# Batches 3 to 7 in runs of nine tokens, their attention products on four array quadrants, in a new order

## The chip, the core and the metric

The kernel runs on one core of a Trainium2 chip. A core has five engines with instruction streams of their own: TensorE (PE; its weight loads are shown apart as PEld), VectorE (DVE), ScalarE (ACT), GpSimd (POOL) and SyncE (SP), and sixteen DMA engines that move data between the chip's memory (DRAM) and SBUF. Matmul results go to PSUM, eight banks of 128 partitions by 512 float32. The metric is the device time of one execution in microseconds (us); a kernel's time is the median of several runs.

## The reference

Two stages follow each other: a linear attention without softmax, normalised per head, and a two-layer network with a leaky activation.

```python
kv = np.einsum('bhsd,bhse->bhde', k, v)        # 8 batches, 8 heads, 576 tokens, 64 dims
out = np.einsum('bhsd,bhde->bhse', q, kv)
rms = np.sqrt(np.mean(out * out, axis=-1, keepdims=True) + 1e-06)
attn = (out / rms * g_norm).astype(np.float32)
x = np.ascontiguousarray(attn.transpose(0, 2, 1, 3)).reshape(4608, 512)
h = x @ w_in                                   # 512 -> 2048
g = np.maximum(h, 0.0) + alpha * np.minimum(h, 0.0)
return (g @ w_out).astype(np.float32)          # 2048 -> 512
```

All inputs and the output are float32 in DRAM; the kernel computes in float16 with float32 sums.

## The kernel before

**Windows and batches.** The network runs over nine windows of 512 tokens (w = 0 to 8, four tiles of 128). A batch has 576 tokens, so windows and batches do not line up: window 3 holds the end of batch 2 and the start of batch 3, and so on. Batches 0 to 2 (below `B_NAT`) go through paths of their own in the first 66 us; the change is about batches 3 to 7.

**Loads.** A batch's q, k and v are loaded by POOL with a cast to float16 into one stage tile each, which every later batch uses again. 512 tokens go as four neighbouring tokens per partition (`load_main`, 128 partitions, runs of 1 KB in DRAM); the remaining 64 tokens go by a load of their own into a small buffer (`load_rem`, runs of 256 B). q comes in two halves by heads. Each load may be held back on POOL by a gate, a one-element copy that waits for a given result.

**Order within a batch.** `place_of` says where a token stands: in batches with an odd number the first 64 tokens are the remainder, in even ones the last 64. Output tokens are permuted accordingly, and `row_pieces`, `grid` and `store_rows` put them back when stored.

**kv product** (`kv_mm`, line 1376): for each of four pairs of heads and each of five token groups, one 128-row matmul per head; the two heads go to the two column halves of the array, 40 matmuls of 128x64 a batch. `kv_copy` (ACT) casts the result into `kv_masked`, once straight and once with partition halves exchanged.

**Transposes of q** (`dma_t`, line 397): SP issues DMA transposes that turn q into `qt_sb`, four of 128x512 from the stage tile and one of 64x512 from the remainder.

**Row products** (`rows_mm`, line 567): for two tiles of a window at a time, q times kv. The contraction is 64 long, so a matmul uses one row half (`half`) of the array; consecutive matmuls alternate between the halves. A tile of main tokens takes 8 matmuls of 64 rows by 128 tokens by 64; a part of 64 remainder tokens takes 8 of its own. ACT then squares 8 pieces per tile (line 627), takes the reciprocal root (637), DVE scales the rows (653, `x_rows`) and SP turns them by DMA into `xt` (665), the input of the network.

**The network.** Groups of four matmuls: `h_ps` (lines 687 and 720, 512 columns wide) for the first layer, `yX`, `yY`, `yZ` (line 940, 256 wide) for the second; some first-layer blocks are computed with seven products instead of eight (`mX`, `mY`, `mV`, line 1286), as the second layer's are.

**The order.** From 66 us on, the instruction stream is written out by hand in a list, `ORDER`. Names in it: `ld.k.4.0` is a load (batch 4, part 0; `@` names its gate), `q.3.2` transpose 2 of batch 3, `kv.7` and `kvc.7` the kv product and its casts, `R.3.1` and `R.3.3` the row products of window 3 for tiles (1, 0) and (3, 2), `q2`/`q3` squares, `rs` reciprocal roots, `n` scaling, `x.3.3` the turn of tile 3 of window 3 into `xt`, `M.w.u` and `Ma.w.0` first-layer groups (`Ma.w.0` and `M.w.0` are one group split in two, since the last tile comes later), `p.w.n.k` second-layer groups, `f.w.s.n` first-layer products, `y` evacuations, `st` stores, `S`, `t` and `a` sums on DVE. Each engine takes its own instructions in the list's order and waits for what they need.

Of the kernel before, what the change touches and what calls it, by code (L numbers as in the profile page):

```python
# [17 lines left out]
def kernel(  # L18
# [11 lines left out]
    nc = tc.nc  # L30
# [103 lines left out]
    mask32 = const_p.tile([P, P], FP32, name="mask32")  # L134
    nc.vector.memset(mask32[:], 0.0)
    nc.vector.memset(mask32[0:64, 0:64], 1.0)
    nc.vector.memset(mask32[64:128, 64:128], 1.0)
    mask16 = const_p.tile([P, P], FP16, name="mask16")
    nc.vector.tensor_copy(out=mask16[:], in_=mask32[:])
    eps_t = const_p.tile([P, 1], FP32, name="eps_t")  # L140
    nc.vector.memset(eps_t[:], 1e-6)
    PAD = P // 2
    qt_sb = [const_p.tile([P, NPAIR, PAD + S + PAD], FP16, name=f"qt_sb{i}") for i in range(2)]
    for t in qt_sb:
        nc.vector.memset(t[:, :, 0:PAD], 0.0)
        nc.vector.memset(t[:, :, PAD + S : PAD + S + PAD], 0.0)

# [12 lines left out]
    NBUF = 3  # L160
    HH = H // 2
    bufs = []
    for i in range(NBUF):
        t = {}
        for nm in ("k", "v", "q") if i < 2 else ("k", "v"):
            n = NT if nm == "q" and i == 0 else 1
            t[nm] = qkv_p.tile([P, n, H, D], FP16, name=f"{nm}sb{i}")
            if i > 0 or nm == "v":
                clears.append(t[nm][REM:P, n - 1, :, :])
        bufs.append(t)  # L170
# [29 lines left out]

    def load_main(b, nm, h0=0, h1=H):
# [9 lines left out]
    def load_q(b, i):  # L211
        load_main(b, "q", i * H // QL, (i + 1) * H // QL)

    def buf_of(b, nm):
        return bufs[b % (2 if nm == "q" else NBUF)][nm]

    def rem_of(b, nm):
        return buf_of(b, nm)[:, TPP if nm == "q" and b % 2 == 0 else 0, :, :]
# [170 lines left out]
    def dma_t(b, ts=tuple(range(NT))):  # L389
        qt = qt_sb[b % 2][:, :, PAD : PAD + S]  # L390
        for t in ts if b >= B_NAT else ():
            n = P if t < TPP else REM
            if t == TPP:
                src = rem_of(b, "q")[0:REM].rearrange("p h d -> p (h d)")
            else:
                src = stages[b, "q"][:, 2 * t : 2 * t + 2].rearrange("p h t d -> p (h t d)")
            nc.sync.dma_start_transpose(
                out=qt_flat(b)[:, t * W : t * W + NC * n].rearrange("p (c n) -> p c n", c=NC),
                in_=src,
            )  # L400
# [12 lines left out]
    def place_of(b, r):  # L413
        if b >= B_NAT and b % 2:
            r = r - REM if r >= REM else r + MAIN
        return divmod(r, P) if r < MAIN else (TPP, r - MAIN)
# [1552 lines left out]
```

## Time and profile before

| what | us |
|---|---|
| median of 3 runs | 272.28 |
| lowest, highest run | 271.85, 273.44 |
| the profiled execution | 271.0 |
| its span, first to last instruction | 269.1 |
| TensorE busy in it | 262.0 |
| VectorE, ScalarE, GpSimd busy | 225.7, 192.3, 85.1 |

The span is what the trace shows; the execution's own time adds what lies before and after. A profile page has numbered parts: busy times, the span in 40 slices, DMA queues, the chain of work that ended last, groups of instructions, DMA issues. A group's line reads: line, engine, operation, output<-inputs, shape, count, then busy us, mean ns of one, and idle time of the engine before them with what ended it. A view of waits reads: engine, what it was about to do, what it waited for, total us, times, longest. A matmul's record (some 190 ns at least) is longer than its share of the array, as matmuls overlap; what one costs is read from how the starts follow each other.

### The profile page before, as it was taken

What the parts mean: (1) busy time and instruction counts of PE and PEld (TensorE: products, weight loads), DVE (VectorE), ACT (ScalarE), POOL (GpSimd) and SP (SyncE); (2) the same over time, 40 slices, a digit from 0 to 9 for tenths busy, and PEclk for the clock granted to TensorE, in tenths of its full rate; (3) what the DMA queues carried; (4) which work ended last, traced back from release to release, by engine and by line L of the source; (5) the groups of instructions that cost most, each with busy time, mean ns of one, the idle gap of its engine ahead of it and who ended that gap; (6) DMA issues with size and microseconds to landing.
All of it is one profiled execution on the core that took longest, in us unless ns stands there. A gap on an engine that the chain in (4) does not pass through costs nothing.

```text
span 269.1 us, 6703 instructions
## 1 busy us (share of the span) xinstructions
PE 262.0 (97%) x2477; PEld 183.1 (68%) x2477; DVE 225.7 (84%) x437; ACT 192.3 (71%) x689; POOL 85.1 (32%) x146
## 2 busy tenths in 40 slices
PE   6999999999999999999999999999999999999994
PEld 2554454456666566886788578866886688678894
DVE  7559966899964998999977997899899988979973
ACT  2567637786579878997889779869988885657500
POOL 8943651513132119411905143511020002401400
PEclk9999999999999999999999999999999999999999
DMA  7999999995989899999999969997550101600233
GB/s 194 198 202 206 196 198 189 181 186 96 225 97 189 126 112 134 177 119 133 175 148 109 129 130 167 105 195 145 117 100 19 23 20 38 204 16 2 78 119 117
DMA packets 75460, 35.75 MB, mean 133 GB/s; under 512 B 42516, under 2 KB 73252, under 8 KB 75428
## 3 DMA queue, kind: packets, MB, share of 16 engines
q0 software_dynamic: 41744, 23.68, 63.7%
q1 hardware_dynamic: 32980, 10.90, 24.7%
q10 hardware_dynamic: 704, 0.75, 0.9%
q8 instruction: 19, 0.31, 0.5%
q14 instruction: 13, 0.11, 0.2%
HBM read 36.71 MB, written 9.44 MB: 171 GB/s over the span
## 4 chain that ended last, share of the span: by engine, by line
PE 87%; DMA 4%; DVE 4%; ACT 2%; SPq 1%; issue 1%; DVEq 0%
PE h_ps L687 25%; PE yY L940 15%; PE yX L940 9%; PE yZ L940 9%; PE mY L1286 8%; PE y L732 5%; PE mV L1286 4%; DMA qt_sb<-qst 3%; PE mX L1286 2%; PE h_ps L720 2%; PE or_ps L567 2%; PE kv_ps L1376 2%; DMA y_sb<-in_g_norm_dram 1%; ACT sq_sb L627 1%; DVE gt L1353 1%; PE ssq_ps L492 1%
## 5 line engine op out<-in xcount | busy, mean ns | idle before, releaser
L687 PE MATMUL h_ps<-xt,w_in_sb 128*128 128x512 f16 x348 | 84.0, 379 | 0.0
L702 DVE SCALAR_TENSOR_TENSOR gt<-m_sb,beta_sb,h_ps 128x512 f16<-128x512 f32 x96 | 68.5, 744 | 12.3 <-ACT m_sb L696 11.5
L696 ACT ACTIVATE m_sb<-h_ps 128x512 f32<-128x512 f32 x96 | 55.4, 605 | 20.7 <-PE h_ps L687 14.8
L940 PEld LDWEIGHTS <-s 128*128 128x128 f16 x496 | 47.9, 98 | 9.5
L687 PEld LDWEIGHTS <-w_in_sb 128*128 128x128 f16 x348 | 33.0, 98 | 31.2 <-issue 0.3
L940 PEld LDWEIGHTS <-gt 128*128 128x128 f16 x384 | 37.3, 98 | 7.2
L627 ACT ACTIVATE sq_sb<-or_ps 128x64 f16<-128x64 f32 x192 | 40.8, 261 | 1.6 <-PE or_ps L567 1.1
L627 ACT ACTIVATION_READ_ACCUMULATOR sq_sb<-or_ps 128x1 f32 x192 | 40.1, 247 | 0.0
L940 PE MATMUL yX<-w_out_sb,gt 128*128 128x256 f16 x256 | 36.8, 273 | 0.0
L940 PE MATMUL yY<-wsum,s 128*128 128x256 f16 x256 | 33.5, 273 | 0.0
L744 POOL DMA_DIRECT2D out_dram<-y_sb x31 | 18.3, 597 | 26.7 <-ACT y_sb L996 16.2
L744 POOL DMA_DIRECT2D out_dram<-y_more x11 | 6.6, 601 | 50.7 <-DVE y_more L1002 30.6
L653 DVE TENSOR_TENSOR x_rows<-or_ps,rstd_r 128x512 f16<-128x512 f32 x27 | 18.2, 686 | 4.2 <-ACT rstd_r L637 3.6
L1353 DVE SCALAR_TENSOR_TENSOR gt<-m_sb,beta_sb,mh 128x256 f16<-128x256 f32 x48 | 20.9, 480 | 0.5 <-ACT m_sb L1346 0.4
L1308 DVE TENSOR_TENSOR mh<-mV,mu 128x512 f32<-128x512 f32 x24 | 16.5, 690 | 5.6 <-ACT mu L1305 3.2
L1448 POOL COPY gate_sb<-gt 1x1 f16<-1x1 f16 x19 | 4.1, 216 | 47.8 <-DVE gt L702 37.4
L940 PE MATMUL yZ<-wsum,s 128*128 128x256 f16 x120 | 17.1, 273 | 0.0
L1305 ACT COPY mu<-mY 128x512 f32<-128x512 f32 x24 | 14.4, 602 | 3.7 <-PE mY L1286 3.7
L1346 ACT ACTIVATE m_sb<-mh 128x512 f32<-128x512 f32 x24 | 15.3, 646 | 2.1 <-DVE mh L1308 2.1
L940 PE MATMUL yY<-wsum,gt 128*128 128x256 f16 x128 | 16.6, 272 | 0.0
L732 PE MATMUL y<-w_out_sb,gt 128*128 128x512 f16 x64 | 16.3, 380 | 0.0
L940 PE MATMUL yZ<-w_out_sb,s 128*128 128x256 f16 x120 | 16.0, 273 | 0.0
(151 smaller groups left out, 433.2 us busy)
## 6 DMA issues: line engine op xcount, KB each, us to landing
kst<-in_k_dram POOLq DMA_DIRECT2D x7, 512.0 KB, 8.3
vst<-in_v_dram POOLq DMA_DIRECT2D x6, 512.0 KB, 8.4
qst<-in_q_dram POOLq DMA_DIRECT2D x10, 256.0 KB, 5.6
w_out_sb<-in_moe_w_out_dram POOLq DMA_DIRECT2D x8, 256.0 KB, 12.2
out_dram<-y_sb POOLq DMA_DIRECT2D x7, 256.0 KB, 4.4
out_dram<-y_sb POOLq DMA_DIRECT2D x12, 128.0 KB, 4.4
out_dram<-y_sb SPq DMA_DIRECT2D x5, 256.0 KB, 2.5
w_in_sb<-in_moe_w_in_dram POOLq DMA_DIRECT2D x2, 512.0 KB, 10.7
```

The source lines that it names most:

```text
L627: nc.scalar.activation(out=sq[:, half, j], in_=o_ps[:, half, j], func=AF.Square, accum_out=ssq[:, half, j : j + 1],)
L653: nc.vector.tensor_tensor(out=xr[:].rearrange("p j h d -> p h j d"), in0=o_ps, in1=rstd[:].unsqueeze(3).to_broadcast([P, 2, NPAIR, D]), op ...
L687: nc.tensor.matmul(out=h_ps[:], lhsT=w_in_blk(c, g), rhs=xts[w][:, c, :], start=(c == 0), stop=(c == NC - 1),)
L696: nc.scalar.activation(out=neg[w, g][:], in_=h_ps[:], func=AF.Relu, scale=-1.0)
L702: nc.vector.scalar_tensor_tensor(out=gts[w, i][:, r, :], in0=neg.pop((w, g))[:], scalar=beta_sb[:, g : g + 1], in1=h_ps[:], op0=ALU.mult, ...
L732: nc.tensor.matmul(out=y[:], lhsT=gt_cols(w, g, a * P, (a + 1) * P), rhs=w_out_blk(g), start=(n == 1), stop=(n == NF),)
L744: engs[store_turn[0] % len(engs)].dma_start(out=dst, in_=src)
L940: nc.tensor.matmul(out=bank, lhsT=lhs, rhs=rhs, start=fresh, stop=(c == NK - 1), skip_group_check=True,)
L1286: nc.tensor.matmul(out=t[bank][:, r, :], lhsT=lhs[:, c, r * P : (r + 1) * P], rhs=rhs[:, c, :], start=(fresh and c == r == 0), stop=(c == ...
L1308: nc.vector.tensor_add(out=h_tile(t, what)[:, :, HW:W], in0=src[:], in1=u[:])
L1346: nc.scalar.activation(out=dst, in_=h, func=AF.Relu, scale=-1.0)
L1353: nc.vector.scalar_tensor_tensor(out=gts[w, i][:, r, cols], in0=m, scalar=beta_sb[:, g : g + 1], in1=h, op0=ALU.mult, op1=ALU.add,)
```

## The change

Batches 3 to 7 are loaded like batch 0: the 128 partitions of a pair of heads each take nine neighbouring tokens of one head (64 partitions per head), 2304 B in one run, in two halves per tensor (`load_runs`). There is no remainder load any more. q's stage tile has a tenth, empty run (zeroed once), so that its 128 x 2560 elements turn in five full transposes. A token's place is now a slot (0 to 8, its run position in `SLOTS`) and a partition (0 to 63).

The kv product takes 64-row matmuls: nine runs, two pairs (column half `c`), two heads (row half `i`), twice, 72 matmuls of 64x64 that go round the four quadrants; the two row halves write to two PSUM banks. Row products take 64 tokens a matmul; a part's slot parity gives its row half, its place in the tile (0 or 64) its column half, and the four parts of two tiles take turns. The slots of the four parts are two even and two odd in all pairs of whole tiles from batch 3 on but one: tiles 3 and 2 of window 7 have slots 8, 8, 4 and 6.

Stores of these batches go in pieces of 64 tokens; where the two tiles of a store have neighbouring slots, two tokens go together. The mask is built in float16, the zero columns beside `qt_sb` are gone, and `ORDER` is written anew. A row product now needs all five transposes of its batch, a load of q all five of the batch before.

```diff
+    def load_runs(b, nm, i):
+        if (b, nm) not in stages:
+            first = nm not in kept
+            stages[b, nm] = stage_for(b, nm, [P, NPAIR, (T0 + (nm == "q")) * D])
+            if nm == "q" and first:
+                nc.vector.memset(stages[b, nm][:, :, T0 * D :], 0.0)
+        n = NPAIR // QL
+        nc.gpsimd.dma_start(
+            out=stages[b, nm][:, i * n : (i + 1) * n, 0 : T0 * D],
+            in_=srcs[nm][b].rearrange("h s d -> (h s d)").rearrange(
+                "(j q r) -> q j r", j=NPAIR, r=T0 * D
+            )[:, i * n : (i + 1) * n, :],
+        )
...
             nc.sync.dma_start_transpose(
-                out=qt_flat(b)[:, t * W : t * W + NC * n].rearrange("p (c n) -> p c n", c=NC),
-                in_=src,
+                out=qt_flat(b)[:, t * W : (t + 1) * W].rearrange("p (c n) -> p c n", c=NC),
+                in_=stages[b, "q"][:].rearrange("p j n -> p (j n)")[:, t * W : (t + 1) * W],
             )
...
+    SLOTS = {
+        3: (8, 0, 2, 1, 3, 4, 6, 5, 7), 4: (0, 2, 1, 3, 4, 6, 5, 7, 8), 5: (8, 5, 7, 0, 2, 1, 3, 4, 6),
+        6: (5, 7, 0, 2, 1, 3, 4, 6, 8), 7: (8, 0, 2, 1, 3, 4, 6, 5, 7),
+    }
...
-                        lhs = qt_flat(b)[part, c : c + n]
-                        rhs = kvs[b][part, half ^ h, j, :]
+                        c = (NT * j + t // 2) * P + h * P0
+                        lhs = qt_flat(b)[part, c : c + P0]
+                        rhs = kvs[b][part, (j + half) % 2, 2 * h + j // 2, :]
...
-        apart = all(len({y[0] for y in x}) == 1 for x in ops)
+        apart = all(x[0] >= B_NAT for i in tiles for x in row_parts(w, i))
+        queues = {}
         for x, i in enumerate(tiles):
-            ots[w, "r", i] = o_ps[:, half] if apart else o_ps[:, :, x]
+            ots[w, "r", i] = o_ps[:, x] if apart else o_ps[:, :, x]
+            for op in row_ops(w, i):
+                half, h, rows, n = op[0], op[1], op[2], op[2].stop - op[2].start
+                key = (rows.start, x) if apart else half
+                rank = 0 if apart else (n, half == h, h) if n < P else (n, 0, 0)
+                queues.setdefault(key, []).append((rank, x, op))
+        queues = [sorted(queues[k], key=lambda y: y[0]) for k in sorted(queues)]
...
+        for n in range(max(map(len, queues))):
+            for y in queues:
...
+    def kv_runs(b):
+        kv_tiles[b] = row_tile([2, H, D], "kv_ps")[:, :, 0 : NPAIR // 2, :]
+        for m in range(NPAIR // 2):
+            for t in range(T0):
+                for c in range(2):
+                    for i in range(2):
+                        k_rows, v_rows = (
+                            stages[b, nm][i * P0 : (i + 1) * P0, 2 * m + c, t * D : (t + 1) * D]
+                            for nm in "kv"
+                        )
+                        nc.tensor.matmul(
+                            out=kv_tiles[b][c * D : (c + 1) * D, i, m, :], lhsT=k_rows, rhs=v_rows,
+                            start=(t == 0), stop=(t == T0 - 1), skip_group_check=True,
+                        )
...
-                needs += [("q", b, x) for x in ((TPP,) if t == TPP else range(TPP) if b >= B_NAT else (t,))]
+                needs += [("q", b, x) for x in ((t,) if b < B_NAT else range(NT))]
...
-            own = ()
-            if nm == "q":
-                n = TPP // QL
-                own = (("q", b - 2, t),) if t == TPP else tuple(("q", b - 1, n * t + i) for i in range(n))
+            own = tuple(("q", b - 1, x) for x in range(NT)) if nm == "q" else ()
...
-            store_engines[0] = (nc.scalar if h == 0 else nc.sync,)
+            store_engines[0] = (nc.scalar, nc.sync)
             store_rows(w * W + P, y_sb[:, 1, half], HC + h * P, HC + (h + 1) * P)
```

The new list's stretches that the prediction speaks of:

```
late.2.0 late.2.2 late.2.1 y.1.seed M.2.1 kv.3 r.2.1 S.1.1.2 M.2.2 s.2.1 S.1.1.1 p.1.2.3
ld.v.4.1@s.2.1 S.1.1.0 r.2.2 M.2.3 a.2.2 kvc.3 s.2.2 M.2.5 S.1.1.3 M.2.6 S.1.2.3 q.3.2 r.2.5
S.1.2.0 S.1.2.2 p.1.6.0 s.2.5 r.2.6 Ma.2.0 q.3.1 S.1.2.1 M.2.0 s.2.6 p.1.6.1 p.1.6.2 q.3.4
p.1.6.3 M.2.10 y.1.u2 q.3.0 r.2.0 M.2.9 r.2.3 s.2.0 p.1.7.0 q.3.3 a.3.4 p.1.7.1 s.2.3
p.1.7.2 p.1.7.3 ld.k.4.0@s.2.6 M.2.4 y.1.u3 y.1.c11 M.2.7 r.2.4 r.2.10 p.2.1.0 s.2.4 r.2.7
p.1.4.0 S.1.4.1 r.2.9 ld.q.4.1@s.2.4 R.3.1 s.2.10 p.1.4.1 q2.3.1 S.1.4.0 p.2.1.1 s.2.9
p.1.4.2 q2.3.0 ld.q.4.0@s.2.5 S.2.3.0 M.2.13 q3.3.1 S.1.4.2 s.2.7 M.2.8 q3.3.0
ld.v.4.0@s.2.2 M.2.11 rs.3.1 rs.3.0 n.3.1 r.2.8 M.2.14 r.2.11 n.3.0 s.2.11 R.3.3 x.3.0
p.1.4.3 q2.3.2 s.2.8 M.2.15 S.1.4.3 y.1.c21 x.3.1 p.2.1.2 q3.3.2 p.1.5.0 p.1.5.1 q2.3.3
p.1.5.2 rs.3.2 p.1.5.3 q3.3.3 n.3.2 M.2.12 y.1.c22 x.3.2 rs.3.3 p.2.1.3 r.2.13 n.3.3 p.1.3.0
y.2.p1 p.1.3.1 s.2.13 x.3.3 r.2.12 p.1.3.2 S.2.1.0 r.2.14 p.2.2.0 s.2.12 p.1.3.3 q.4.2
p.2.2.1 y.1.c12 R.4.1 S.2.2.0 Ma.3.0 y.2.seed q.4.3 r.2.15 S.2.3.1 p.2.6.0 q2.4.0 p.2.6.1
s.2.15 q.4.0 M.3.0 M.3.1 q2.4.1 s.2.14 ld.k.4.1@s.2.15 t.3.1 r.3.0 M.3.2 q.4.1 S.2.1.1 r.3.1
...
p.5.6.1 t.6.2 r.6.7 x.7.1 S.5.2.1 kv.7 s.6.1 p.5.6.2 kvc.7 st.3.c12 p.5.6.3 s.6.4 p.5.2.1
s.6.6 y.5.u2 R.7.3 S.5.3.0 M.6.5 st.4.c12 q2.7.2 S.5.3.1 p.5.2.2 q2.7.3 t.6.3 x.7.0 p.5.2.3
```

More of the change, by code (lines that the diff above doesn't have):

```diff
@@ L156 @@
         )
-    NBUF = 3
     HH = H // 2
[L162 to L170, printed above, removed]
+    bufs = {}
+    for b in range(1, B_NAT):
+        for nm in "kvq":
+            n = NT if nm == "q" and b == 2 else 1
+            t = bufs[b, nm] = qkv_p.tile([P, n, H, D], FP16, name=f"{nm}sb{b}")
+            if n == 1:
+                clears.append(t[REM:P, 0, :, :])
     def clear(n):
@@ L534, in row_ops @@
                 for h in range(2):
-                    n = rows.stop - rows.start
-                    half = h if b < B_NAT or t == TPP else t % 2
+                    half = h if b < B_NAT else t % 2
                     part = slice(half * D, (half + 1) * D)
```

286 lines of the change are left out of this document (123 added, 163 removed).

## The prediction

> **What bounds the kernel now.** I read the page first: shares of the engines, the 40 slices and the shares of the chain that ended last.
>
> ```profile
> PE 262.0 (97%) x2477; PEld 183.1 (68%) x2477; DVE 225.7 (84%) x437; ACT 192.3 (71%) x689; POOL 85.1 (32%) x146
> ...
> PE   6999999999999999999999999999999999999994
> ...
> DMA  7999999995989899999999969997550101600233
> ...
> PE 87%; DMA 4%; DVE 4%; ACT 2%; SPq 1%; issue 1%; DVEq 0%
> ```
>
> TensorE is full from the second slice to the last but one, at full clock (the 1.00 in the counts further down). A transfer or a slower neighbour costs time only where it leaves TensorE without work; a saved matmul counts directly. The view of waits, for PE alone, says how much there is to win:
>
> ```profile
> PE warm_ps L316 <- DVE y_sb L133: 1.5, 1, 1.5
> PE alpha_ps L1061 <- DMA y_sb<-in_g_norm_dram: 0.7, 1, 0.7
> PE kv_ps L1376 <- DVE gt L702: 0.5, 1, 0.5
> PE or_ps L567 <- DVE x_rows L653: 0.4, 1, 0.4
> PE or_ps L567 <- DMA qt_sb<-qst: 0.3, 1, 0.3
> ```
>
> The first two belong to the start, before the edited part, and alpha_ps waits for a DMA that the edit leaves alone. So all that waiting costs in the middle is three waits, 0.5 + 0.4 + 0.3 = 1.2 us, each ahead of an attention block. The blocks, and the units of work around them, stand in the chain in order of time (start, us, what; h_ps and yY in their groups of four matmuls):
>
> ```profile
> 69.10 0.86 PE h_ps L687 x4
> ...
> 77.62 6.91 DMA qt_sb<-qst
> ...
> 88.29 0.82 ACT sq_sb L627 x8
> ...
> 99.75 0.44 PE yY L940 x4
> 100.19 0.75 PE kv_ps L1376 x40
> ...
> 184.39 0.60 PE or_ps L567 x24
> ```
>
> A kv product costs 0.75 us, five of them (batches 3 to 7) are edited. Nine of the twelve row blocks of windows 3 to 8 have 16 matmuls, three have 24 (0.60 us each). A block of 16, from the chain cut to 165 to 182 us:
>
> ```profile
> 170.31 0.34 PE or_ps L567 x16
> ```
>
> **Matmuls on quadrants.** A kv product becomes 72 matmuls of 64x64 instead of 40 of 128x64; a row block 32 instead of 16. Whether that costs anything depends on the pace when all four quadrants take turns. No kv product before does that, but the 24-blocks do in places: there 64 tokens are computed on both row halves into both column halves. Counting the matmuls of line 567 begun from 184.30 on (us, PE busy and count, clock, DMA):
>
> ```profile
> 184.30:184.41 0.11, 0.09 (x10) 1.00 0.95 335
> 184.30:184.44 0.14, 0.12 (x14) 1.00 1.03 366
> ```
>
> From 0.41 to 0.44 four are begun in 30 ns: 7.5 ns each at four quadrants. The other bound is the pace of two column halves, line 1376 counted from 66.60:
>
> ```profile
> 66.60:66.72 0.12, 0.06 (x4) 1.00 0.77 73
> 66.60:66.82 0.22, 0.16 (x10) 1.00 1.05 49
> ```
>
> 6 in 0.10 us, 16.7 ns each. I take 7.5, since that row shows the very form. With 0.12 us for entering and leaving a block (0.75 less 38 times 16.7 ns), kv is 72 x 7.5 ns + 0.12 = 0.66 us, 0.09 less: 5 x -0.09 = **-0.4**. At 16.7 ns it is 1.32 us, +2.9 in all.
>
> Row blocks: 32 x 7.5 ns + 0.12 = 0.36 against 0.34, nine of them: +0.2. The block of window 5's tiles 3 and 2 goes from 0.60 to 0.36: -0.2. Window 3's tiles 1 and 0 keep 24 matmuls. Window 7's tiles 3 and 2 are the exception: the slots of all its four half tiles are even, so all 32 lie on one row half and use two quadrants. The nearest row is the second part of window 5's block, eight matmuls on one row half:
>
> ```profile
> 131.50:131.80 0.30, 0.27 (x16) 1.00 1.43 272
> 131.50:132.02 0.52, 0.49 (x24) 1.00 1.72 227
> ```
>
> 8 in 0.22 us, 28 ns each. If column halves overlap, 16 x 28 ns + 0.12 = 0.57, no change; if nothing overlaps, 1.0 us, +0.4. I take the first. Row blocks together: **0**; at 16.7 ns a block is 0.65, +2.9 in all.
>
> The Trainium skill, "TensorE: Matmul & The Clock Gate", section "The mechanism", says that a weight load overlaps matmuls in flight only when its row group differs. By that, window 7's block would show every one of its 32 loads, priced in the rival below; the trace speaks against it, since the eight matmuls of the last fence, on one row half, come 28 ns apart though a load takes 107 ns:
>
> ```profile
> L567 PEld LDWEIGHTS <-qt_sb 64*64 64x64 f16 x48 | 0.7, 107 | 0.6 <-issue 0.6
> ```
>
> **The waits that go.** The new order moves kv.7 away from what it waited for (between R.7.1 and kv.7 stand six h_ps groups and fifteen groups of four products, before three and thirteen), R.4.1 away from R.3.3 (thirteen product groups and two h_ps groups; before six and four: 7.4 against 6.1 us), and has all transposes of batch 3 issued ahead of R.3.1. All three waits can go: **-1.2**; at worst 0.
>
> **The waits that come.** Four places are tighter than before.
>
> R.3.3 needs the PSUM of R.3.1 free. Between them the new order has three product groups and four h_ps groups, 3 x 0.44 + 4 x 0.86 = 4.8 us. Meanwhile ACT squares 16 pieces, at 0.82 per four 3.3 us, and DVE scales both tiles:
>
> ```profile
> 82.49 1.37 DVE L653 TENSOR_TENSOR x_rows<-or_ps,rstd_r 128x512 f16<-128x512 f32 x2 [2.36 <-ACT rstd_r L637]
> ```
>
> With 0.4 us each for starting and for rstd_r (an estimate, from the same stretch, 78.2 to 83.9) 3.3 + 0.8 + 1.4 = 5.5: a wait of **+0.7** (0 to 1.2).
>
> R.7.3 stands only three product groups, 1.3 us, behind kv.7, and needs kv_masked, copied by ACT in two pieces:
>
> ```profile
> 69.03 0.37 ACT L1391 CAST kv_masked<-kv_ps 128x256 f16<-128x256 f32 x1
> 69.41 0.74 ACT L1394 CAST kv_masked<-kv_ps 64x256 f16<-64x256 f32 x2
> ```
>
> 1.1 us and a start of 0.3: **+0.1** (0 to 0.7, if a copy for another product is ahead on ACT).
>
> R.3.1 now holds the first 64 tokens of batch 3, which sat in the one remainder transpose; they now sit in the last slot, which spans the transposes, so it waits for all. SP issues them one after another; rows of the queue and of landings:
>
> ```profile
> 71.50 2.12 SPq L397 DMA_TRANSPOSE qt_sb<-qst  x1
> 73.78 1.17 SPq L397 DMA_TRANSPOSE qt_sb<-qsb  x1
> 75.06 3.82 SPq L397 DMA_TRANSPOSE qt_sb<-qst  x3
> ```
> ```profile
> xt<-x_rows SPq DMA_TRANSPOSE x27, 3.2
> qt_sb<-qst SPq DMA_TRANSPOSE x20, 5.0
> ```
>
> Starting at 71.7 at 1.27 us each, the fifth is issued at 76.8 and lands at 80.0 (3.2 us, the median of the xt transposes) to 81.8 (5.0). R.3.1 comes at 66.7 + nine h_ps groups, ten and a half product groups, kv and one split h_ps group, 14.0 us = 80.7. A wait of 0 to 1.1; I take **+0.3**, nearer the quick end, because the loads of batch 4's k are gated on a transpose that stands just ahead of the fifth.
>
> M.3.0 needs x.3.3, the last turned tile of window 3. Behind it the new order has four product groups, R.4.1, three quarters of an h_ps group and two product groups, 3.6 us (before 5.0); the landing takes 3.2 to 5.0: **+0.2** (0 to 1.4).
>
> **What costs nothing.** Seven loads per batch become six, on POOL, which is busy 32%. If that cover failed, one more issue would be 0.6 us on POOL:
>
> ```profile
> L744 POOL DMA_DIRECT2D out_dram<-y_sb x31 | 18.3, 597 | 26.7 <-ACT y_sb L996 16.2
> ```
>
> Stores of batches 3 to 7 are cut into pieces of 64 rows; POOL has 7 more instructions, SP 6. On SP they stand ahead of the x_rows transposes, whose closest first use is the one just priced. Five memsets and one conversion fewer on DVE lie in the start, where alpha_ps waits for a DMA anyway; two fewer, and one more for the empty run of q's stage, lie under products. At the end the last stores become twice as many, spread over ACT, SP and POOL:
>
> ```profile
> 264.61 1.52 ACTq L744 DMA_DIRECT2D out_dram<-y_sb  x3
> ```
>
> Three issues take 0.4 to 0.5 us each; the last half tile finds its queue busy for about **+0.1** (0 to 0.8, if POOL's piece lands last).
>
> **Sum**, against the profiled execution's own 271.0 us (269.1 span and 1.9 around it): -0.4 + 0 - 1.2 + 0.7 + 0.1 + 0.3 + 0.2 + 0.1 = -0.2. The median of the runs is 272.28, 1.3 above that execution; taken as an equal shift, 272.1.
>
> **Rivals.**
> 1. *Faster*: the planned order holds, none of the new waits comes (-1.3) and the three old ones were worth 0.1 more each, for what a block loses in starting up again. -0.2 - 1.3 - 0.3 = -1.8: 270.5. For it: each new wait is under a microsecond. Against: four near ties must all fall well.
> 2. *Late transposes* (the other side): the five transposes land as the slow one of the trace, 6.91 us after issue, because loads share the DMA engines (the DMA row is at 9 there). The fifth lands at 83.7, R.3.1 waits 3.0 us instead of 0.3; R.5.3, behind its last transpose by four h_ps and four product groups and kv, 5.9 us, waits 1.0. +3.7: 275.8. It decides from a landing of about 5.8 us. Against it: larger runs in the loads leave the queues sooner.
> 3. *The quadrants don't overlap over a long run*: 16.7 ns each, so the work the change describes is not done at once: +3.3 on kv, +2.9 on rows, 278.3. Against: the row with four in 30 ns, though only for some fourteen matmuls.
> 4. *Weights exposed on one row half* in R.7.3: 32 x (107 + 28) ns = 4.3 instead of 0.6 us, +3.7: 275.8. This is what the rule weighed above would make of it. Against: the 28 ns row.
>
> **How the numbers follow.** A measurement here tells about 0.5%, 1.4 us, from no change. The forecast, within that, 0.38, with its own range 270.9 to 273.6; rival 1, 0.34; rival 2, 0.20; rival 3, 0.06; rival 4, 0.02. So faster 0.34, same 0.38, slower 0.28. The range for 8 in 10 reaches from 269.8 (rival 1, with 0.7 for the spread of the runs) to 275.8 (rival 2), leaving out rival 3 and the edges.
>
> **What would show it.** Right: kv blocks near 0.66 us and row blocks near 0.36 in the chain; in PE's waits no kv_ps on gt, but or_ps on x_rows near 85 us; a span of 268 to 270. Wrong: kv above 1 us (rival 3), a wait of or_ps on DMA of over 2 us near 81 us (rival 2), R.7.3 above 1.5 us (rival 4), or a wait at a place that I did not name, for which the sum has no term.

## The result, and the profile after

| | us |
|---|---|
| before, median of 6 runs (lowest, highest) | 272.06 (270.69, 273.44) |
| after, median of 6 runs (lowest, highest) | 275.16 (274.37, 277.04) |
| ratio after/before, 95% interval | 1.0116 (1.007 to 1.0163) |
| the profiled execution after, its span | 275.3, 273.2 |

The change makes the kernel 3 us slower. The profiled execution spans 273.2 us where the one before spanned 269.1: 4.1 us to account for. The page of the changed kernel, busy times first, then the 40 slices of TensorE and the shares of the chain that ended last:

```profile
PE 263.3 (96%) x2797; PEld 183.7 (67%) x2797; DVE 223.4 (82%) x430; ACT 192.7 (71%) x689; POOL 84.9 (31%) x153
...
PE   6999999999999899999999999999999999999993
...
PE 74%; DMA 9%; ACT 6%; DVE 5%; POOL 2%; issue 2%; DVEq 0%; POOLq 0%
```

TensorE is as busy as before (263.3 against 262.0 us), but its share of the chain fell from 87% to 74%: other engines and transfers now stand in the path. One slice in the first half, the fourteenth (89 to 96 us), is below 9. The waits of PE, without the one of the warm-up at the very start, say where:

```profile
PE alpha_ps L1068 <- DMA y_sb<-in_g_norm_dram: 1.0, 1, 1.0
PE yZ L947 <- DVE y_sb L1009: 0.6, 1, 0.6
PE h_ps L690 <- DVE gt L705: 0.6, 1, 0.6
PE h_ps L690 <- DMA w_in_sb<-in_moe_w_in_dram: 0.5, 1, 0.5
PE h_ps L723 <- DMA xt<-x_rows: 0.5, 2, 0.3
PE or_ps L570 <- DVE x_rows L656: 0.2, 1, 0.2
```

The three waits that the edit was to remove (kv_ps on gt, or_ps on x_rows ahead of R.4.1, or_ps on DMA) are gone. In their place stand h_ps on gt (M.2.1, at 67 us), yZ on y_sb (p.1.3.0, 94 us), h_ps on xt (0.3 of it Ma.3.0, 98 us) and or_ps on x_rows (R.3.3, 88 us). The chain in order of time (start us, us, what) shows the last three as one piece:

```profile
82.31 1.60 PE or_ps L570 x24
...
83.94 3.39 ACT sq_sb L630 x32
...
88.99 0.48 PE or_ps L570 x32
...
90.90 1.65 ACT sq_sb L630 x16
...
94.20 0.11 DVE y_sb L1009
94.31 3.98 DMA xt<-x_rows
...
98.42 0.81 PE h_ps L723 x4
```

From 84 to 98 us the path runs through squares, scaling, R.3.3, squares, an addition and a turn of x; TensorE's own work there is beside the path. The first row holds a second surprise: R.3.1, the block of window 3's tiles 1 and 0, takes 1.60 us. The count of its matmuls begun from 82.20 on (us, PE busy and count, loads, clock, DMA):

```profile
82.20:82.46 0.26, 0.22 (x12) 0.21 (x12) 1.00 1.46 182
...
82.20:83.40 1.20, 1.16 (x19) 0.88 (x19) 1.00 1.13 161
82.20:83.80 1.60, 1.56 (x24) 1.16 (x24) 1.00 1.08 160
```

Twelve begin in the first quarter microsecond; the next seven take 0.94 us, 134 ns each. Before, the whole block stood between two rows of TensorE 0.49 us apart (start, us, operation):

```profile
77.71 0.56 PE L567 MATMUL or_ps<-kv_masked,qt_sb 64*64 64x64 f16 x24
78.20 0.60 PE L687 MATMUL h_ps<-xt,w_in_sb 128*128 128x512 f16 x2
```

It also began 4.5 us earlier then, at 77.7 instead of 82.2. Last, the end. The timeline of before, the last matmuls, the last addition and the stores:

```profile
264.56 1.06 PE L935 MATMUL yZ<-w_out_sb,s 128*128 128x128 f16 x16
264.61 1.52 ACTq L744 DMA_DIRECT2D out_dram<-y_sb  x3
...
265.65 0.29 DVE L1686 TENSOR_TENSOR y_sb<-yZ,u 128x128 f32<-128x128 f32 x1 [0.16 <-PE yZ L935]
265.97 0.34 SPq L744 DMA_DIRECT2D out_dram<-y_sb  x1
```

and of the changed kernel:

```profile
267.64 1.06 PE L942 MATMUL yZ<-w_out_sb,s 128*128 128x128 f16 x16
267.70 2.71 ACTq L747 DMA_DIRECT2D out_dram<-y_sb  x4
...
267.96 0.61 POOL L747 DMA_DIRECT2D out_dram<-y_sb  x1 [7.50 <-DVE y_sb L1007]
268.30 1.82 SPq L747 DMA_DIRECT2D out_dram<-y_sb  x3
...
268.94 0.29 DVE L1706 TENSOR_TENSOR y_sb<-yZ,u 128x128 f32<-128x128 f32 x1 [0.30 <-DMA out_dram<-y_sb]
```

Before, the span ends 3.5 us behind the last matmul (269.1 less 264.56 + 1.06); now 4.5 (273.2 less 267.64 + 1.06). Eight issues, each of 64 rows and some 0.6 us (three on SP in 1.82), take the place of four of 128 rows at 0.34 to 0.5, and ACT's queue is still issuing at 270.4, 1.2 us behind the last addition. The work of the edit itself is as quick as it was meant to be: a kv product, a row block and R.7.3 in the chain:

```profile
69.14 0.71 PE kv_ps L1402 x72
...
132.93 0.38 PE or_ps L570 x32
...
188.78 0.62 PE or_ps L570 x32
```

### The profile page after: what moved, and what is told of

It is laid out like the page before. It is cut to its first block, busy times and chain, and to the rows that moved or that the text cites. A ratio compares the mean times of both kernels' runs of the same rounds, so it can differ in the third digit from the quotient of the medians.

```text
span 273.2 us, 7370 instructions
## 1 busy us (share of the span) xinstructions
PE 263.3 (96%) x2797; PEld 183.7 (67%) x2797; DVE 223.4 (82%) x430; ACT 192.7 (71%) x689; POOL 84.9 (31%) x153
## 3 DMA queue, kind: packets, MB, share of 16 engines
HBM read 36.71 MB, written 9.44 MB: 169 GB/s over the span
## 4 chain that ended last, share of the span: by engine, by line
PE 74%; DMA 9%; ACT 6%; DVE 5%; POOL 2%; issue 2%; DVEq 0%; POOLq 0%
PE h_ps L690 23%; PE yY L947 11%; PE yX L947 8%; PE yZ L947 7%; PE mY L1291 6%; PE y L735 5%; DMA xt<-x_rows 5%; ACT sq_sb L630 4%; DMA w_in_sb<-in_moe_w_in_dram 3%; PE mV L1291 3%; PE h_ps L723 2%; PE or_ps L570 2%; DVE gt L705 2%; PE mX L1291 2%; PE kv_ps L1402 1%
## 5 line engine op out<-in xcount | busy, mean ns | idle before, releaser
L690 PE MATMUL h_ps<-xt,w_in_sb 128*128 128x512 f16 x348 | 82.4, 379 | 1.3 <-DVE gt L705 0.6
L690 PEld LDWEIGHTS <-w_in_sb 128*128 128x128 f16 x348 | 33.4, 98 | 34.5 <-issue 1.1
L747 POOL DMA_DIRECT2D out_dram<-y_sb x43 | 24.3, 571 | 82.5 <-DVE y_sb L1009 42.0
L1351 ACT ACTIVATE m_sb<-mh 128x512 f32<-128x512 f32 x24 | 15.3, 637 | 4.5 <-DVE mh L1313 4.4
L947 PE MATMUL yY<-wsum,gt 128*128 128x256 f16 x128 | 17.4, 273 | 0.1
L1473 POOL COPY gate_sb<-gt 1x1 f16<-1x1 f16 x14 | 2.9, 207 | 45.1 <-DVE gt L705 40.0
L947 PE MATMUL yZ<-wsum,s 128*128 128x256 f16 x120 | 16.4, 273 | 0.0
L1291 PEld LDWEIGHTS <-w_in_sb 128*128 128x128 f16 x144 | 13.9, 98 | 2.3
```

The costliest lines, as they stand in the source:

```text
L690: nc.tensor.matmul(out=h_ps[:], lhsT=w_in_blk(c, g), rhs=xts[w][:, c, :], start=(c == 0), stop=(c == NC - 1),)
L747: engs[store_turn[0] % len(engs)].dma_start(out=dst, in_=src)
L947: nc.tensor.matmul(out=bank, lhsT=lhs, rhs=rhs, start=fresh, stop=(c == NK - 1), skip_group_check=True,)
L1291: nc.tensor.matmul(out=t[bank][:, r, :], lhsT=lhs[:, c, r * P : (r + 1) * P], rhs=rhs[:, c, :], start=(fresh and c == r == 0), stop=(c == ...
L1351: nc.scalar.activation(out=dst, in_=h, func=AF.Relu, scale=-1.0)
```

## The experiments

A ratio is to the kernel before, run on the same chip in the same series; the differences in us below are differences of ratios times 271.7. Between two runs the intervals leave some 1 to 1.6 us either way, so where a difference is smaller than that, the traces have to decide. "The stretch at the end" is the span's end less the end of the last matmul row, as just reckoned.

**The changed kernel again** (no edit).

> The changed kernel once more, beside the others on the same chip: about 275.2 us, 1.01 of before. If the 0.8 us that the changed kernel's profile lost in its first 17 us (alpha_ps 1.0 against 0.7, h_ps on w_in 0.5) is chance, this profile starts like the one of before; if it belongs to the change, the two waits stand here again with the same lengths.

275.48 us, ratio 1.0145 (1.0108 to 1.0183): this, in the series of the next runs, is what they are held against. Its waits:

```profile
PE h_ps L723 <- DVE mh L1313: 0.8, 1, 0.8
PE alpha_ps L1068 <- DMA y_sb<-in_g_norm_dram: 0.7, 1, 0.7
PE yZ L947 <- DVE y_sb L1009: 0.6, 1, 0.6
PE h_ps L690 <- DVE gt L705: 0.6, 1, 0.6
PE h_ps L723 <- DVE s L865: 0.5, 1, 0.5
PE or_ps L570 <- DVE x_rows L656: 0.2, 1, 0.2
```

alpha_ps waits 0.7 as before the change and h_ps on w_in not at all: the loss of 0.8 us at the start of the first profile was chance. (R.3.1 began at 81.6 here, so 0.6 of the 4.5 us by which it came later was that chance.) The waits at gt, yZ, Ma.3.0 (here put down to s) and R.3.3 stand again. The 0.8 on mh is new and lies at 149 us, outside all that follows; it came in some profiles and not in others.

**Sizes together.** In R.3.1 the old code sorted by tokens per matmul; the new one shifts one row half's queue against the other's, so that matmuls of 128 and 64 tokens take turns.

```diff
+        turns = [y[n] for n in range(max(map(len, queues))) for y in queues if n < len(y)]
         if not apart:
-            queues.sort(key=len)
-            queues[0][:0] = [None] * ((len(queues[1]) - len(queues[0])) // 2)
+            turns = []
+            for size in (P0, P):
+                sized = [[y for y in q if y[2][2].stop - y[2][2].start == size] for q in queues]
+                turns += [y[n] for n in range(max(map(len, sized))) for y in sized if n < len(y)]
...
```

> The changed kernel, but window 3's block of tiles 1 and 0 issues its 16 matmuls of 64 tokens first and its 8 of 128 tokens behind them: one change of tile size in place of eight. Theory 'sizes' (each change between 64x64 and 64x128 costs 125 to 146 ns): the block at 82 us takes about 0.5 us from its first to its last start instead of 1.46, and the run is 0.9 to 1.0 us faster than the changed kernel: 274.2. Rival 'pace' (the block is slow because both halves' weights come from different tiles): the block keeps over 1.2 us and the time stays at 275.2. Rival 'slack' (the block gets short, but R.3.3 or the first layer of window 3 then waits longer for ACT and the turns): block 0.5, time at least 274.9.

274.23 us, 1.011 (1.0062 to 1.0157), 0.95 us less than the changed kernel. The block in the chain:

```profile
81.62 0.64 PE or_ps L569 x24
```

0.64 instead of 1.60: 'sizes' holds and 'pace' falls. As a time, 0.95 us lies within the intervals, so against 'slack' stands the trace: the waits behind the block are no longer than before (yZ 0.6, Ma.3.0 0.4, R.3.3 0.2), and Ma.3.0 begins 15.3 us behind the block's start instead of 16.2 and 16.4 in the two profiles of the changed kernel.

**More changes of size, in the kernel before.** The opposite edit in the three blocks of 24 of the old code:

```diff
-            n = next((n for n, y in enumerate(left) if was and y[1] != was[1]), 0)
+            other = [n for n, y in enumerate(left) if was and y[1] != was[1]]
+            sized = [n for n in other if left[n][3].stop - left[n][3].start != was[3].stop - was[3].start]
+            n = (sized or other or [0])[0]
```

> The kernel before the change, but its three row blocks with 16 matmuls of 64 tokens and 8 of 128 take a size in turn (64, 128, 64, 128 while there are both), still alternating between the row halves: some 16 changes of size in a block in place of one. Theory 'sizes': 125 to 146 ns each, so each block takes about 2.0 us longer: 0.37 becomes 2.3 to 2.5 us from its first to its last start, and the kernel up to 6 us slower, 276 to 278. Rival 'pace' (the 1.46 us belong to the new layout's operands, not to the changes): blocks under 0.6 us, time as before, 271.7.

278.06 us, 1.0281 (1.0244 to 1.0318): 7.6 us, somewhat over the 6 expected. R.3.1 of this kernel in its chain:

```profile
77.82 2.45 PE or_ps L569 x24
```

2.45 where the block took 0.49, so 2.0 for fifteen more changes of size, 130 ns each. The other two blocks of 24 go from 0.6 to 2.5; the three make 5.7 of the 7.6. A wait of 1.3 us for a load ahead of a kv product, which this profile also has, is not explained by the edit and may be the rest. Operands and layout are those of before: the price belongs to the change of size.

**The stores of the end, whole.**

```diff
+    def last_out(w, r, h, src, subs, c0=0, c1=256):
+        late = out[w * W : (w + 1) * W, :].rearrange("(p t) m -> p t m", t=4)
+        if len(subs) == 2:
+            put(late[:, 2 * r : 2 * r + 2, h * HC : (h + 1) * HC], src)
+        else:
+            put(late[:, 2 * r + subs[0], h * HC + c0 : h * HC + c1], src)
...
-        quad_out(w, int(what[1]) - 1, int(what[2]) - 1, y_sb, subs)
+        r, h = int(what[1]) - 1, int(what[2]) - 1
+        last_out(w, r, h, y_sb[:] if len(subs) == 2 else y_sb[:, subs[0], :], subs)
...
```

This kernel writes the last window's tokens to rows that are not theirs: some rows of the output are written twice and others not at all. The bytes written are as many as before (9.44 MB), so it can be measured, but it is no version to use.

> The changed kernel, but the stores of the last window go out as before the change, 128 partitions at a time (five stores in place of ten); tokens of the last window land in other rows, so this part of the output is permuted. Theory 'tail' (twice as many stores of 64 rows, 0.55 to 0.66 us of issue each, and a tile of y_sb that comes free later make the stretch behind the last matmul 4.5 instead of 3.5 us): that stretch goes back to 3.5 us and the time to 274.1 to 274.4. Rival (the end is set by the landing of any store, whatever its form): 4.2 to 4.5 us, time 275.0.

274.19 us, 1.0102 (1.0063 to 1.0142): 1.2 us less. Its timeline at the end (span 273.4):

```profile
269.00 1.06 PE L949 MATMUL yZ<-w_out_sb,s 128*128 128x128 f16 x16
269.06 1.47 ACTq L747 DMA_DIRECT2D out_dram<-y_sb  x3
...
270.45 0.34 SPq L747 DMA_DIRECT2D out_dram<-y_sb  x1
```

Three issues in 1.47 us, the last of 0.34, and 3.3 us from the last matmul to the end, where the changed kernel had 4.5 and 4.4. 'tail' holds by the trace; the gain in time agrees with it, with intervals that overlap. (The span is no shorter than that of the changed kernel because in this profile the last matmuls begin 1.0 to 1.4 us later; the stretch at the end does not contain that.)

**The end, spread otherwise.** With the sizes together, both last halves in one y_sb tile, c21's pieces on SP and POOL instead of ACT and POOL, c12's dealt to SP and ACT in another order, and

```diff
-            store_engines[0] = (nc.scalar, nc.sync)
+            store_engines[0], store_turn[0] = ((nc.scalar, nc.gpsimd), (nc.sync, nc.scalar))[h], -1
```

> The changed kernel with the sizes of the block of window 3 put together (as in the run of that) and, beside it, the last stores spread otherwise: both halves of the last half tile in one tile of y_sb, so that DVE's last addition waits for no store; no queue but SP's and ACT's ends with two pieces of the last data. All stores keep their 64 rows. Theory 'tail': DVE's last addition starts at its data, 0.3 us earlier, and the last issue ends some 0.3 to 0.5 earlier, so the stretch behind the last matmul is 4.0 to 4.2 instead of 4.45 us and the time 273.7 to 274.0. Rival: a piece on POOL lands last and eats it: 4.4 us or more, 274.2.

274.41 us, 1.0129 (1.0099 to 1.016): no better than sizes alone (1.011). The addition no longer waits, but the stretch is 5.1 us (4.4 with the sizes alone): the end of the chain now lies on POOL.

```profile
266.32 0.61 POOL out_dram L746
...
267.27 0.55 POOLq L1973
```

**The order: the old list.** The changed kernel takes the list of before, with only what the new loads and transposes demand (part 4 of a load becomes part 1, `q.4.4` and `q.6.4` move up to their batch's others, R.7.3 waits for its transposes to be issued).

> The changed kernel with the old list of the order (a load's part 4 becomes part 1, the load of q's remainder goes, the last transpose of batches 4 and 6 comes right behind the other four, R.7.3 and two squares are held back until their needs are issued). Theory 'order' (the new list brought the new waits: h_ps on gt at 67 us, yZ on y_sb at 94, Ma.3.0 on xt at 98, together about 2 us beyond what it removed): those waits go and the old three of 0.5, 0.4 and 0.3 come back; 274.0 to 274.5. Rival 'new form' (the new layout makes the same waits under any list, since needs moved): about 275.2 or, with a late turn for R.3.1 or R.7.3, up to 277.

289.39 us, 1.0632 (1.0585 to 1.0679). The chain around R.3.1 and the first row of PE's waits:

```profile
80.28 4.92 DMA qt_sb<-qst
...
85.23 2.17 PE or_ps L570 x20
```
```profile
PE or_ps L570 <- DMA qt_sb<-qst: 11.9, 4, 4.7
```

Both theories miss: under the old list R.3.1 and R.7.3 stand in front of transposes that they now need whole, and wait 11.9 us between them. The clock does the rest. Around the wait of 4.7 us ahead of 85.23 the counts of TensorE read (us, PE busy and count, clock, DMA)

```profile
82.00:83.00 1.00, 0.00 (x0) 0.76 1.05 132
88.00:92.00 4.00, 4.00 (x14) 0.50 1.13 179
93.00:94.00 1.00, 1.00 (x11) 1.00 0.11 18
```

The granted clock falls to 0.50 while TensorE waits and stays there for 7 us after it works again, in which a group of four h_ps takes up to 1.82 us instead of 0.86; behind the waits at R.7.3 it is 0.50 again, from 206 to 212 us. About 13 us of work at half the clock lose about 6 (an estimate from these rows). With the waits that is 18 us, about what this profile is longer than that of the changed kernel (290.7 against 273.2). The new list is not the fault; it is what the new layout demands, and it pays for it by putting R.3.1 some 4 us later.

**One wait at a time.** kv.3 ahead of M.2.1:

```diff
-late.2.0 late.2.2 late.2.1 y.1.seed M.2.1 kv.3 r.2.1 ...
+late.2.0 late.2.2 late.2.1 y.1.seed kv.3 M.2.1 r.2.1 ...
```

> The changed kernel with one step moved in the list: kv.3 ahead of M.2.1, as the old list had it, instead of behind. Theory 'order': the wait of h_ps on gt at 67 us (0.6) is there only because M.2.1 stands first and finds its PSUM not yet read; kv.3's 0.7 us cover it and nothing else moves: the wait goes, 274.6 to 274.9. Rival 'chain': the stretch from R.3.1 on is set by ACT and DVE, so the time comes back as a longer wait of R.3.3, yZ or Ma.3.0: the wait at 67 us goes, time 275.2 to 275.5. Rival 'kv waits': kv.3 finds the same PSUM or its loads late, a kv_ps wait of 0.5 or more in its place.

275.08 us, 1.0149 (1.0121 to 1.0177). The wait at 67 us (0.6) is gone, but 0.3 stands at another h_ps group, at 71.7 us; yZ, Ma.3.0 and R.3.3 wait 0.6, 0.6 and 0.2, hardly other than before. What is gained is 0.3 us at most, too little to see in the time, and this run doesn't decide between 'order' and 'chain'. Then y.1.c22 ahead of n.3.2:

```diff
-p.1.5.2 rs.3.2 p.1.5.3 q3.3.3 n.3.2 M.2.12 y.1.c22 ...
+p.1.5.2 rs.3.2 p.1.5.3 y.1.c22 q3.3.3 n.3.2 M.2.12 ...
```

> The changed kernel with one step moved in the list: y.1.c22 (DVE) ahead of n.3.2, the scaling of a tile, behind which it stands on DVE. Theory 'order': p.1.3.0 waits 0.6 us at 93 us because the read of its PSUM bank stands behind n.3.2, and n.3.2 waits for ACT's sixteen squares; moved ahead, the yZ wait goes; x.3.2 starts some 0.3 us later, which is not the last tile; time 274.6 to 274.9, if Ma.3.0's wait on xt (0.4 to 0.6) doesn't grow by the same 0.6. Rival 'chain': the chain of squares, scaling and turns sets Ma.3.0; PE only comes to it earlier and waits 1.2 us there: time 275.2 to 275.5.

275.84 us, 1.0167 (1.014 to 1.0193). No gain. The yZ wait is gone as meant, and PE's list begins

```profile
PE h_ps L723 <- DMA xt<-x_rows: 1.9, 2, 1.3
```

The longer one, 1.3, stands at Ma.3.0, where it was 0.3 and 0.5 in the two profiles of the changed kernel (the other 0.6 lies at 149 us): TensorE only came to Ma.3.0 earlier. That is what 'chain' said.

**R.3.1 earlier.**

```diff
...
-p.1.7.2 p.1.7.3 ld.k.4.0@s.2.6 M.2.4 y.1.u3 y.1.c11 M.2.7 r.2.4 r.2.10 p.2.1.0 s.2.4 r.2.7
-p.1.4.0 S.1.4.1 r.2.9 ld.q.4.1@s.2.4 R.3.1 s.2.10 p.1.4.1 q2.3.1
+p.1.7.2 p.1.7.3 R.3.1 ld.k.4.0@s.2.6 M.2.4 q2.3.1 y.1.u3 y.1.c11 M.2.7 q2.3.0 r.2.4 r.2.10 p.2.1.0
+s.2.4 r.2.7 q3.3.1 p.1.4.0 S.1.4.1 r.2.9 ld.q.4.1@s.2.4 s.2.10 p.1.4.1 q3.3.0
...
```

> The changed kernel with another stretch of the list: the transposes of batch 3 go in the order 0, 1, 2, 3, 4 (the first two need only the first half of q), R.3.1 stands four groups (2.6 us of TensorE's work) earlier, R.3.3 two first-layer groups earlier, and their squares, scalings and turns with them. Theory 'chain' (R.3.1 has to wait for all five transposes, so it starts at 82 us in place of 78, and from there squares, scaling, R.3.3, squares, scaling and the turn set when window 3's first layer can begin; the waits at R.3.3, yZ and Ma.3.0, together some 1.6 us, are this one delay): R.3.1 starts at 78.8 to 79.5, the waits at yZ and Ma.3.0 go or shrink below 0.5 together, 273.9 to 274.4. Rival 'DVE and ACT are full there' (the waits only move): the sum of PE's waits between 79 and 100 us stays above 1.3 and the time at 275. Rival 'late transposes' (the fifth still lands at 80.4): R.3.1 waits 1 us or more itself, 275 to 276.

278.96 us, 1.0261 (1.0224 to 1.0299), and with the other parts beside it

> Put together: the sizes of window 3's block sorted, kv.3 ahead of M.2.1, the early R.3.1 and R.3.3, and both last halves in one tile of y_sb; all 64-row stores stay. If the parts add up (1.0 for the sizes, 1.0 for the chain, 0.3 for kv.3 once the chain no longer eats it, 0.3 at the end): 275.3 less 2.6 = 272.7, still 1 us behind the kernel before, about what the tail's stores keep. If the chain eats kv.3's part: 273.0. Rival (parts don't add): 274 or more.

279.22 us, 1.0269 (1.0228 to 1.0311). Both theories miss by more than 4 us; 'DVE and ACT are full there' had the growing waits right and the time 4 us too low. In the first run, R.3.1 began at 78.9 us as planned, but the transposes still landed at 80.1, so it waited 0.6 us between its matmuls. The chain from there on, and the first row of PE's waits:

```profile
83.74 0.83 ACT sq_sb L630 x8
84.57 1.46 ACT m_sb L699 x3
```
```profile
PE h_ps L690 <- DVE gt L705: 3.9, 4, 2.0
```

Squares now stood ahead of the evacuations (m_sb) of first-layer groups, and these held TensorE for 3.3 us (0.6 of the 3.9 is the wait at 67 us, which was there). ACT is full there, 4.00 of 4.00 us from 82 to 86, and moving its work only moves the wait. Whether R.3.1 as such can come earlier with gain, this doesn't tell.

**Shorter squares.** So the chain was cut where it doesn't get longer elsewhere: tiles 3 and 2 of window 3 are squared in one ACT instruction and summed by DVE, a form that the code has for window 2.

```diff
     def RED(w):
-        return (0, 1, 3) if w == 2 else red(w)
+        return (0, 1, 3) if w == 2 else (2, 3) if w == 3 else red(w)
```

> The changed kernel, list untouched, but for tiles 3 and 2 of window 3 ACT squares a whole tile in one instruction and DVE sums it (as window 2's tiles do: 0.59 us on ACT and 0.68 us on DVE a tile, in place of eight pairs of small ACT instructions, some 1.7 us a tile). It is the test that the early R.3.1 was not, since nothing stands ahead of other evacuations. Theory 'chain' (squares, scaling and turns between R.3.3 and Ma.3.0 set the waits at yZ and Ma.3.0): the scaling of tile 2 comes over 1 us earlier, both waits (0.6 and 0.4 to 0.6) go, 274.0 to 274.4. Rival (the waits come from DVE's own queue, which now has 1.4 us more): both stay or grow, 275.3 to 276.

273.38 us, 1.0083 (1.0055 to 1.0111): 1.7 us less than the changed kernel, though in another series. The chain from R.3.3 on:

```profile
88.36 0.44 PE or_ps L570 x32
...
90.65 1.75 PE yZ L947 x16
```

It has returned to TensorE and stays there up to Ma.3.0; the waits at yZ and Ma.3.0, 1.1 us in all, are gone; so is the 0.8 at 149 us, which came and went by itself. But is that the change's loss, or a gain that any version has? The same line in the kernel before, twice:

> The kernel before the change with the short squares for tiles 3 and 2 of window 3 (one ACT instruction and a sum on DVE a tile), nothing else. Theory 'chain' (only the late R.3.1 of the change makes squares, scaling and turns the limit): at most the 0.4 us that R.4.1 waits for x_rows go, and DVE has 1.4 us more; 271.4 to 272.2, the time of the kernel before. Rival (a gain that any version has): 270.0 to 270.4.

> The kernel before with the short squares of window 3's tiles 3 and 2, once more. Theory 'chain': nothing that can be told, ratio 0.996 to 1.002. Rival (a gain that any version has, of the size that the changed kernel showed): ratio 0.994 or less.

270.56 us, 0.9977 (0.9951 to 1.0003), then 269.93 us, 0.9956 (0.9935 to 0.9978). Both lie between the two forecasts. So 0.6 to 1.2 us of the 1.7 are to be had before the change too, and 'chain' as I put it, with nothing to gain in the kernel before, falls. The second profile has no wait of PE left but the two of the start: or_ps on x_rows (R.4.1, 0.4) is gone in both, and so is kv_ps on gt (0.5), while or_ps on DMA stood at 0.5 in the first and is gone in the second. Only R.4.1 lies behind the squares that were shortened; kv_ps waited at 180 us, and why that wait went too isn't shown. By these figures the change made the stretch of window 3's squares 0.5 to 1.1 us worse; the intervals allow more and less.

**The parts together.** Sizes together, kv.3 first, short squares, both last halves in one tile:

> Put together without moving R.3.1: block of window 3 sorted by size, kv.3 ahead of M.2.1, the short squares of tiles 3 and 2 of window 3, both last halves in one tile of y_sb. If the parts add up: 275.4 less 1.1 (sizes) less 1.1 (chain) less 0.3 (kv.3, no longer eaten behind) less 0.2 (end) = 272.7, about 1 us behind the kernel before, which is what the 64-row stores of the end keep. Rival (the parts overlap: one delay counted twice): 273.5 or more.

272.57 us, 1.0051 (1.0025 to 1.0077). Then, on top of it, one last store instead of two halves, and that with the one POOL store of the last window moved to SP:

```diff
-            store_engines[0] = (nc.scalar, nc.sync)
-            store_rows(w * W + P, y_sb[:, 1, half], HC + h * P, HC + (h + 1) * P)
+        store_rows(w * W + P, y_sb[:, 1, :], HC, 2 * HC)
...
-            store_engines[0] = (nc.scalar, nc.gpsimd, nc.sync, nc.gpsimd)
+            store_engines[0] = (nc.scalar, nc.sync)
```

> The combined kernel (sizes sorted, kv.3 first, short squares, one tile of y_sb), and the last half tile is stored once behind both additions instead of in two halves of 128 columns: two last stores of 64 rows by 256 columns, one on SP, one on ACT, in place of four. Theory 'tail' (what ends last is the queue of 0.6 us issues): the last issue starts at the last addition's end, some 0.6 us earlier, the stretch behind the last matmul is 3.9 to 4.1 instead of 4.5 us, 272.0 to 272.2. Rival (landing of the longer last pieces takes it back): 4.4 or more, 272.6.

> The combined kernel with one last store (e12), but no store of the last window on GpSimd: the piece goes to SP, whose queue is free then. Theory 'drain' (GpSimd's drain ends 3.7 us after its store's issue and holds the end, 0.4 us behind SP's last wait): the end follows SP's last wait, the stretch behind the last matmul is 3.7 to 3.9 in place of 4.3 us, and the time 0.4 to 0.5 less than e12's, 272.2 to 272.5 beside a kernel before of 271.3. Rival (the drain waits for something else that stays): 4.2 or more.

272.91 us, 1.0057 (1.0037 to 1.0077), and 272.31 us, 1.003 (1.0007 to 1.0053). The stretch at the end was 4.5 us with the parts together, then 4.3, then 4.0: shorter each time, but less than either theory said. Two stores fewer gave nothing that can be told; the POOL store gave 0.3 in the trace, and its effect on the time lies within the intervals. Last, the parts with the whole stores of before (again with tokens in rows that are not theirs):

> The combined kernel (sizes sorted, kv.3 first, short squares of window 3's tiles 3 and 2) with the last window's stores of 128 partitions as before the change; tokens of the last window land in other rows, so this part of the output is permuted. Theory 'tail': 1.0 to 1.1 us less than the combined kernel, 271.4 to 271.6, the time of the kernel before within 0.3; sizes, chain and tail are then the whole loss. Rival: a further loss that none of these covers, 272.2 or more.

271.96 us, 1.0016 (0.9995 to 1.0036): between the two forecasts, and level with the kernel before, with a stretch of 3.6 us. Together the parts win back 3.5 of the 3.9 us that the changed kernel lost in its series (1.0145). Alone, they gained 0.95 (sizes), 1.2 (end) and 1.7 us (squares), 3.85 in all; with over 1 us of uncertainty in each, that this sum comes so close is luck. The books close only against the kernel before as it was: held against that kernel with the same short squares (0.9977 and 0.9956), this one is still 1.1 to 1.6 us behind. Two waits that its view of PE still has are a part of that, h_ps on gt (0.3, at 73 us) and or_ps on x_rows (0.2, R.3.3). Where the rest lies these runs don't settle.

## Why the prediction was wrong

It forecast no change, 272.1 us, and the kernel became 3 us slower, clear of the noise. That 275.2 still lies inside the range (269.8 to 275.8) is luck: the upper end was the price of rival 2, and neither that nor rival 4, priced at 275.8 too, took place. Between the two profiles the sum, -0.2, should have been +4.1. Its terms, with what the first profile measured:

| term | predicted | measured |
|---|---|---|
| kv products, five | -0.4 | -0.2 (0.71 against 0.75 each) |
| row blocks but R.3.1 | 0 | +0.2 (nine at 0.38 against 0.34; 0.60 to 0.38 once; R.7.3 0.62) |
| R.3.1 | 0 ("keep 24 matmuls") | +1.1 (1.60 against 0.49) |
| waits that go | -1.2 | -1.2 |
| waits that come | +1.3 | +1.9 (0.6, 0.6, 0.5, 0.2) |
| the end | +0.1 | +1.0 |
| the start | 0 | +0.8, chance |

These make 3.6 of the 4.1; where the other 0.5 lies isn't shown (what TensorE loses around each wait, beyond the row of the view, is a guess).

**Right by its own steps.** The quadrants: 72 matmuls in 0.71 us (0.66 forecast), a block of 32 in 0.38 (0.36). Two column halves of one row half do overlap: R.7.3 took 0.62 (0.57 to 0.60 forecast), so rivals 3 (278.3) and 4 (275.8) fell. By the rule that was weighed there (the Trainium skill, "TensorE: Matmul & The Clock Gate", section "The mechanism") it would have been 4.3 us (the prediction's estimate); the trace disagrees: the block's 32 loads, on one row half, have records of 110 ns and begin two per 32 ns. All three old waits went. R.3.3 on x_rows came where it was forecast, at 0.2 instead of 0.7; R.3.1 did not wait for transposes, so rival 2 fell too, though the old list shows its mechanism at full size. Rival 1 was right about the old waits and wrong about the new ones.

**The step that failed first: "Window 3's tiles 1 and 0 keep 24 matmuls", costed at nothing.** The number of matmuls was the wrong thing to count. Their order changed: the code for blocks that are not `apart` pads one queue, and sizes 64 and 128 alternate. Each change costs 125 to 146 ns in the record of starts, nine in place of one. The old trace held the price, since every block of 24 has one such change; it was there as a part of 0.60 us and I did not take it apart. The prediction counts window 5's block and has 16 matmuls begun by 131.80. The same 16 had begun by 131.70, and the next, of the other size, comes 125 ns behind the last of them (us, PE busy and count, clock, DMA):

```profile
131.50:131.70 0.20, 0.17 (x16) 1.00 1.25 282
```

Put in order of size, the same 24 matmuls of the changed kernel took 0.64. That such a change is not free, the Trainium skill says in words, "TensorEngine Tiling (Array Packing)", section "Key Properties": changing the tiling mode drains TensorE. The traces agree in that a change costs time, and put a figure to it, 130 ns a change over the fifteen added in the kernel before.

**The end, +0.1 for +1.0.** The step priced twice as many issues at 0.4 to 0.5 us, the price of 128-row stores. A 64-row store took 0.6, and it counted only the last queue's delay, not that an earlier store holds a y_sb tile which the last addition needs (0.3 us). The bound of 0.8 "if POOL's piece lands last" was for a different mechanism.

**Waits that come.** The sum was 0.6 short, and the places were half wrong: R.7.3, R.3.1 and M.3.0 didn't wait (Ma.3.0, just ahead, did); M.2.1 (now ahead of kv.3) and p.1.3.0 did, and had no term. I costed each wait by the work between two neighbours on TensorE and asked too little what else stands in ACT's and DVE's queues: p.1.3.0 waits for a read behind n.3.2, which waits for sixteen squares. yZ and Ma.3.0 look like two waits and were one chain behind R.3.3, as the move of y.1.c22 (yZ's wait went to Ma.3.0) and the short squares (both went) show.

**Rival 2's other half.** That R.3.1 needs all five transposes was seen; only a wait of R.3.1 itself was priced. The list had already paid by putting it some 4 us later, and less time was then left for what follows it. That the waits behind R.3.3 come from this lateness is an inference: the one run with R.3.1 earlier lost time for another reason.

## What to carry to other kernels

Price a matmul block by the order of its tile sizes, not only by its count: keep equal sizes together. When a layout change makes an early step need more transfers, price the stretch from that step to its last consumer, not just the wait in front of it, and treat neighbouring small waits as one chain until a single move shows otherwise. Before a large change for a microsecond of waits, try the one line that shortens the chain: here it took the kernel before to 270.6 and 269.9 us in two series, the second clearly ahead of both versions (0.9956, 0.9935 to 0.9978).

## What was not expected of the hardware

A change between 64x64 and 64x128 matmuls takes TensorE 125 to 146 ns from one start to the next, where neighbours of one size are at most 46 ns apart. Stores of 64 rows take SP's and ACT's queues some 0.6 us each, longer than stores of 128 rows with the same or more bytes (0.34 to 0.5). Why the smaller store is the dearer one stays open; the two kinds also differ in the pattern of rows that they write in DRAM. POOL takes part in the end long after its last store: with its last issue at 267.3 us, the end came 5.1 us behind the last matmul instead of 4.4 (other stores differ too between these two); without any store there in the last window it came 4.0 behind it instead of 4.3. And after a wait of 4.7 us TensorE worked another 7 us at a granted clock of 0.50.
